# Seven block products for batches 1 and 2, with the sums of weights moved forward and batch 3 loaded into the first buffers

## The chip, the cores and the metric

The kernel runs on one core of one Trainium2 chip. The metric is the device time of one execution in microseconds (us). A core has a matrix engine (PE in the profile, with its weight loads as PEld), VectorE (DVE), ScalarE (ACT), GpSimd (POOL) and SyncE (SP, which here only issues transfers). Each engine works through its own queue of instructions in order; they wait for one another by semaphores.

## What is computed

Eight batches of linear attention with 8 heads, 576 positions and 64 numbers for each head, followed by an MLP mixer. Cut to what matters:

```
q_p, k_p = phi(q), phi(k)             # phi(x) = x + 1 for x > 0, exp(x) otherwise
kv  = einsum('bhsd,bhse->bhde', k_p, v)
num = einsum('bhsd,bhde->bhse', q_p, kv)
den = einsum('bhsd,bhd->bhs', q_p, k_p.sum(axis=2)) + 1e-6
x   = num / den                       # as [batch, 576, 512]
u   = x + token_mix(x)                # relu(x^T w_tok1) w_tok2, transposed back
out = u + relu(u @ w_ch1) @ w_ch2     # w_ch1 is 512 x 1536, w_ch2 is 1536 x 512
```

The change is about the last product, `relu(u @ w_ch1) @ w_ch2`, and about what has to be ready for it.

## The kernel before

The 576 positions of a batch are four tiles of 128 rows and a tail of 64. The tails of two neighbouring batches share one tile. Matrix operands are bfloat16, the sums in PSUM (eight banks of 512 floats) are float32.

**Stages and pieces.** The program is an order written out by hand. For each batch `n` there is a stage: a list `big` of pieces of matrix work of that batch, and a list `fill` of `(s, function)`. `run(big, fill)` emits piece 0, then what fill has at 0, then piece 1, and so on. Since engines work in order, this order is the order in every queue. The pieces of a stage are:

- `mm3(n, mc)` for 12 values of `mc` (L520): a 128-column slice of `relu(u @ w_ch1)`, four matmuls of 512 columns; ScalarE, or VectorE where `dve` is set, writes it from PSUM to `cr` (L532, L535).
- for odd `n`, three pieces `mm3_tail` (L537): the same for the shared tail.
- the product with `w_ch2`. For batches 0 to 2 it is `mm4(p, t, ...)` (L548): for a tile of rows 12 matmuls of 512 columns, cut into three pieces. For batches from 3 on (`FIRST = 3`, L595) it is `m4s(n)` (L713): 14 pieces of six matmuls of 256 columns.
- for odd `n`, three pieces of `mm4` for tile 8, the shared tail.

The stage named after batch 1 does `mm3` of batch 1, the `mm4` of batch 1's four tiles and the tail of batches 0 and 1 (L921). The stage of batch 2 does `mm3` and `mm4` of batch 2, and so on.

**The seven block products.** With the rows in even and odd tiles and the inner dimension in halves, `cr` is a 2 x 2 block matrix; so is `wc2` (w_ch2 in SBUF). Instead of eight products of blocks, `pair_product` (L680) makes seven, of sums of blocks. Four sums of blocks of `cr` are made for each batch by `row_sums(n, which, k0, m)` on VectorE (L621) and lie in `sb`. Four sums of blocks of the weights are made once, by `weight_sums` on GpSimd (L605), and lie in `tb`; a float32 helper `tf` serves three of them. Product 6 needs `sb[1]` and `tb[1]`, product 5 `sb[0]` and `tb[0]`, product 7 `sb[2]` and `tb[2]`, product 3 `sb[3]`, product 4 `tb[3]`; the order is 1, 2, 6, 5, 7, 3, 4. Three PSUM tiles X, Z, Y hold them. `pair_copy` (ScalarE, L695) saves an intermediate X or Y in `part`, `pair_end` (L698) adds the residual `u` on VectorE (L702) and the saved part on GpSimd (L704), `pair_put` (L706) sends the output off.

**Buffers.** `raw[nm, 0]` and `raw[nm, 1]` are two sets of float32 buffers for q, k and v. `rb(n)` (L123) says which set a batch is loaded into. `sb`, `tb`, `tf` and two of the `part` tiles have no space of their own: they lie in `raw["k", 1]`, `raw["q", 1]` and `raw["v", 1]` (L596 to L600) and in the spent `w2`. So seven products can be used only when the second set of buffers is free of inputs.

**What prepares a batch.** `phi_exp` (ScalarE, L148), `phi_add` (VectorE, L154) and `phi_end` (VectorE, L162) turn the loaded q or k, half a batch each, into `qp` or `kp`. `vcast` (L173) turns v into bfloat16. `kv(n)` (L181) multiplies kp and v in two groups of 36 small matmuls, the second of which uses the second halves. `qtr_dma` transposes q by a transfer. `nd_all(n)` (L249, "nd") makes numerators and denominators, and VectorE writes `x`. Then `mm1` (token mixing, L296), `mm2` in two parts a and b (L307), and transposing transfers `uta`, `utb` (L508), which give the next stage its input.

Of the kernel before, what the change touches and what calls it, by code (L numbers as in the profile page):

```python
# [12 lines left out]
ALU = mybir.AluOpType  # L13
# [5 lines left out]
def kernel(  # L19
# [20 lines left out]
    nc = tc.nc  # L40

    B, H, S, D = q.shape
# [11 lines left out]
    NCH = DCH // 128  # L54
# [63 lines left out]
    def after(ins, other):  # L118
        if other is not None:
            tc.add_manual_dep(ins.ins, other.ins.name, sync_dep, reason="order of transfers")  # L120
        return ins

    def rb(n):  # L123
        return n % 2 if n < 4 else 0

    def load(nm, n, c, gate=None):
        src_ = src[nm][n].rearrange("(j a) (p t) d -> (a p) j (t d)", a=2, t=T)
# [38 lines left out]
    def phi(nm, n, c):  # L166
        phi_exp(nm, n, 2 * c, 2)
        phi_add(nm, n, 2 * c, 2)
        phi_end(nm, n, 2 * c, 2)

    def vcast(n, c, copy=nc.scalar.copy):
        js = slice(2 * c, 2 * c + 2)
        copy(out=vs[:, js, :, 0:D],  # L173
             in_=raw["v", rb(n)][:, js].rearrange("p j (t d) -> p j t d", t=T))
# [41 lines left out]
    def qtr_dma(n):  # L216
        for a in range(2):
            nc.sync.dma_start_transpose(
                out=qT[n % 2][:, 2 * TD * a:2 * TD * (a + 1)].rearrange("p (f s) -> p f s", s=D),
                in_=qp[half[a]].rearrange("p c t i d -> p (c t i d)"))  # L220
# [299 lines left out]
    def mm3(n, mc, kjs=range(NDM), dve=False):  # L520
        b = n % 2
        if kjs[0] == 0:
            part_of[mc] = bank(None if n == 0 else (
                (0, 1, 0, 1, 2, 3, 0, 1, 2, 3, 0, 1) if n > 1 else
                (3, 5, 7, 1, 3, 0, 2, 1, 3, 0, 1, 0))[mc])
        ps = part_of[mc]
        for kj in kjs:
            nc.tensor.matmul(out=ps, lhsT=wc1[:, kj, 128 * mc:128 * mc + 128],  # L528
                             rhs=uT[b][:, :, kj],
                             start=(kj == 0), stop=(kj == NDM - 1))  # L530
        if kjs[-1] == NDM - 1 and dve:
            nc.vector.tensor_scalar(out=cr[b][:, mc, :], in0=ps, scalar1=0.0, scalar2=None,  # L532
                                    op0=ALU.max)
        elif kjs[-1] == NDM - 1:
            nc.scalar.activation(out=cr[b][:, mc, :], in_=ps, func=AF.Relu)  # L535

    def mm3_tail(i, late=True):  # L537
        ps = bank(((2, 3, 0) if late else (1, 2, 3))[i]).rearrange("p (m s) -> p m s", m=4)
        for m in range(4):
            mc = 4 * i + m  # L540
            for kj in range(NDM):
                nc.tensor.matmul(out=ps[:, m], lhsT=wc1[:, kj, 128 * mc:128 * mc + 128],  # L542
                                 rhs=uTt[:, kj, :], start=(kj == 0), stop=(kj == NDM - 1))
        nc.scalar.activation(out=crt[:, 4 * i:4 * i + 4, :], in_=ps, func=AF.Relu)
# [44 lines left out]
    KH = NCH // 2  # L589
# [2 lines left out]
        t = raw[nm, b].rearrange("p j f -> p (j f)").bitcast(BF16)  # L592
        return t[:, 1536 * i:1536 * (i + 1)]

    FIRST = 3  # L595
    tb = [bf("k", 1, i).rearrange("p (k c) -> p k c", k=KH) for i in range(3)] + [  # L596
        bf("q", 1, 0).rearrange("p (k c) -> p k c", k=KH)]
    tf = raw["q", 1].rearrange("p j f -> p (j f)")[:, 768:2304].rearrange("p (k c) -> p k c", k=KH)
# [3 lines left out]
    def wblock(i, j):  # L602
        return wc2[:, KH * i:KH * (i + 1), 256 * j:256 * (j + 1)]

    def weight_sums(k0, m):  # L605
        first = [live["phi"]]
        ks = slice(k0, k0 + m)
        b11, b12, b21, b22 = [wblock(i, j)[:, ks] for i in range(2) for j in range(2)]
        sub = lambda o, x_, y_: after(nc.gpsimd.tensor_tensor(
            out=o[:, ks], in0=x_, in1=y_, op=ALU.subtract), first.pop() if first else None)  # L610
        sub(tf, b12, b11)
        sub(tb[0], b12, b11)
        sub(tb[1], b22, tf[:, ks])
        sub(tb[2], b22, b12)
        sub(tf, b22, tf[:, ks])
        sub(tb[3], b21, tf[:, ks])

    def ablock(n, i, e):
        return cr[n % 2].rearrange("p k (j e s) -> p k j e s", j=2, e=2)[:, KH * i:KH * (i + 1), :, e]
# [93 lines left out]
    def m4s(n):  # L713
        if n + 1 < B:
            return [lambda i=i, j=j: pair_product(n, i, j) for i in ORDER for j in range(2)]
        out_ = []
        for e in LAST:
            out_ += [lambda e=e: product(n, e[1], e[0])] if e else m4(n // 2, [8])
        return out_

    def prep_k(n, g, copy=nc.scalar.copy):
        phi("k", n, g)
        vcast(n, g, copy)

    def k_exp(n):
        for g in range(2):
            phi_exp("k", n, 2 * g, 2)

    def load_all(n, nms):
        if n < B:  # L730
            for nm in nms:
                for g in range(2):
                    load(nm, n, g)
# [170 lines left out]
                 (en, lambda nm=nm, c=c: phi_end(nm, 1, 2 * c, 2))]  # L904
    late = [("vc", lambda: vcast(1, 0)), ("vc", lambda: vcast(1, 1, nc.vector.tensor_copy))]
    fill += [(21, lambda g=g: phi("q", 2, g)) for g in range(2)]
    fill += [(22, lambda: qtr_dma(2)), (22, lambda: load_all(3, "qkv"))]
    first = steps(1)
    for nm, fn in first[1:2] + late + first[2:3] + first[0:1] + first[3:]:
        fill += [(at0[nm], fn)]  # L910
# [7 lines left out]
    for mc in range(3):  # L918
        mm3(1, mc, range(0, 2))
    utr_tail(0)  # L920
    big = [lambda mc=mc: mm3(1, mc, range(2, 4)) for mc in range(3)] + [lambda mc=mc: mm3(1, mc, dve=mc in (5, 8)) for mc in range(3, NCH)] + [  # L921
        lambda i=i: mm3_tail(i, False) for i in range(3)] + m4(0, [4, 5, 6, 7, 8])
    at1 = {"nd": 10, "mm1": 16, "mm2a": 18, "mm2b": 20, "uta": 18, "utb": 20}
    fill = [(s, lambda g=g: phi("k", 2, g)) for g, s in ((0, 0), (1, 2))]
    fill += [(4, lambda: vcast(2, 0)), (5, lambda: vcast(2, 1, nc.vector.tensor_copy))]
    fill += [(8, lambda: kv(2, range(2)))]
    fill += [(at1[nm], fn) for nm, fn in steps(2)]
    fill += [(s, lambda g=g: phi("q", 3, g)) for g, s in ((0, 13), (1, 14))]
    fill += [(6, lambda: load_all(4, "k")), (15, lambda: qtr_dma(3)), (22, lambda: load_all(4, "qv"))]
    fill += [(s, lambda g=g: prep_k(3, g)) for g, s in ((0, 17), (1, 21))]  # L930
    fill += [(22, lambda: k_exp(4)), (22, lambda: weight_sums(0, 2)), (25, lambda: kv(3, range(2)))]
    run(big, sorted(fill, key=lambda e: e[0]))

    for n in range(2, B - 1):
        p, b = divmod(n, 2)
        blocks = n >= FIRST
        big = m3(n) + (m3t if b else []) + (m4s(n) if blocks else m4(p, [0, 1, 2, 3])) + (
            m4(p, [8]) if b else [])
        b0 = 15 if b else 12
        todo = dict(steps(n + 1))  # L940
        fill = []
        put = lambda s, fn: fill.append((s, fn))
        at = lambda s, *nms: [put(s, todo.pop(nm)) for nm in nms if nm in todo]
        sums = lambda s, w, k0, m: put(s, lambda: row_sums(n, w, k0, m)) if blocks else None
        on = lambda s, fn, *a: put(s, lambda: fn(*a)) if blocks else None
        more = n + 2 < B
        at(1, "nd")
        if more:
            for g in range(2):
                put(2, lambda g=g: phi_add("k", n + 2, 2 * g, 2))  # L950
                put(3 + g, lambda g=g: phi_end("k", n + 2, 2 * g, 2))
            put(5, lambda: load_all(n + 3, "k"))
            for g in range(2):
                put(7, lambda g=g: phi_exp("q", n + 2, 2 * g, 2))
            for g in range(2):
                put(8 + g, lambda g=g: phi_add("q", n + 2, 2 * g, 2))
                put(9 + g, lambda g=g: phi_end("q", n + 2, 2 * g, 2))
            put(10, lambda: qtr_dma(n + 2))
        at(7, "mm1")
        if n + 1 == FIRST:  # L960
            for i in (1, 2):
                put(10, lambda i=i: weight_sums(2 * i, 2))
        for s, k0 in ((11, 0), (12, 3)):
            for w in (1, 2):
                sums(s, w, k0, 3)
        at(13, "mm2a", "uta")
        sums(14, 3, 0, KH)
        at(b0 + 3 - b, "mm2b", "utb")
        sums(b0 + 4 - b, 4, 0, KH)
        on(b0 + 1, pair_copy, 0)  # L970
        if more:
            for g in range(2):
                put(b0 + 2 + g, lambda g=g: vcast(n + 2, g))
        on(b0 + 4 - b, pair_end, n, "Z", 0, 0, 0)
        on(b0 + 5, pair_copy, 1)
        at(b0 + 6, "mm2t", "utt")
        put(b0 + 6, lambda: load_all(n + 3, "qv"))
        on(b0 + 7, pair_copy, 2)
        if n + 3 < B:
            put(b0 + 8, lambda: k_exp(n + 3))  # L980
        if more:
            put(b0 + 9, lambda: kv(n + 2, range(2)))
        on(b0 + 9, pair_end, n, "X", 1, 1, 2)
        on(b0 + 11, pair_end, n, "Y", 0, 1, 1)
        on(b0 + 13, pair_end, n, "X", 1, 0)
        on(b0 + 13, pair_put, n)
        assert not todo, todo
        run(big, sorted(fill, key=lambda e: e[0]))

# [34 lines left out]
```

## Time and profile before

| | before |
|---|---|
| time, median of 3 (lowest to highest) | 254.04 us (253.87 to 254.38) |
| span of the profiled execution | 252.8 us |
| PE busy | 244.1 us, 97% of the span |
| DVE, ACT, POOL busy | 161.3, 138.3, 68.0 us |
| granted TensorE clock | 1.00 |

PE busy for 97% of the span says that there are hardly any gaps between its instructions, not that each of them is at its best. The engines beside it have much idle time on average, but it is unevenly spread. The profile is read here mostly by stage: in the chain of work that ended last, the stage of batch 1 begins at about 54 us, that of batch 2 at 85.66, of batch 3 at 112.56 and of batch 4 at 142.89. A name such as `k_raw` in a row is a buffer of the program; where weight sums or row sums lie in it, the row shows the buffer's name.

### The profile page before, as it was taken

To read this page: it belongs to the slowest core of one execution; us is meant where nothing else is said; L and a number is where in the kernel's file an instruction comes from. 1 tells how busy PE (TensorE), PEld (TensorE's weight loads), DVE (VectorE), ACT (ScalarE), POOL (GpSimd) and SP (SyncE) were. 2 spreads that over 40 slices of the span, in tenths; PEclk is the share of its full clock that TensorE was granted. 3 is DMA by queue.
4 is the path that set the end of the run, shared out by engine and by line. 5 is a ranking of instruction groups with operands and counts; after the bars stand their busy time and mean duration, and the time that the engine had idled before them with its cause. 6 is when DMAs were issued, how large, how long until landed. Compare 5 with 4: busy or idle time off the path is not lost.

```text
span 252.8 us, 5704 instructions
## 1 busy us (share of the span) xinstructions
PE 244.1 (97%) x2358; PEld 144.6 (57%) x2358; DVE 161.3 (64%) x282; ACT 138.3 (55%) x218; POOL 68.0 (27%) x84
## 2 busy tenths in 40 slices
PE   7689999999999999999999999999999999999993
PEld 3474455554744444444588545774578545764872
DVE  5855877876876394648854398939864444833543
ACT  4674782469684369416967168566863165137300
POOL 9670120120005904981003500150004500160000
PEclk9999999999999999999999999999999999999999
DMA  6999999899938966459786957769252540435034
GB/s 248 262 203 263 364 233 337 304 269 340 377 94 146 325 223 223 104 163 342 272 126 178 327 136 204 151 200 346 41 114 44 111 100 0 86 62 124 3 93 114
DMA packets 49769, 48.37 MB, mean 191 GB/s; under 512 B 30096, under 2 KB 35600, under 8 KB 49744
## 3 DMA queue, kind: packets, MB, share of 16 engines
q1 hardware_dynamic: 41568, 34.87, 46.6%
q0 software_dynamic: 7632, 12.49, 22.6%
q10 hardware_dynamic: 544, 0.66, 1.1%
q8 instruction: 18, 0.29, 0.4%
q14 instruction: 7, 0.06, 0.1%
HBM read 35.85 MB, written 9.44 MB: 179 GB/s over the span
## 4 chain that ended last, share of the span: by engine, by line
PE 90%; DMA 3%; ACT 2%; DVE 2%; issue 1%; SPq 0%; DVEq 0%; ACTq 0%
PE ps L528 33%; PE ps L555 16%; PE ps L691 15%; PE ps L302 6%; PE ps L542 4%; PE ps L315 4%; PE ps L644 4%; DMA q_raw<-in_q_dram 3%; PE ps L188 2%; PE ps L258 2%; PE ps L463 1%; PE ps L473 1%; PE ps L354 1%; PE ps L336 1%; PE ps L229 0%
## 5 line engine op out<-in xcount | busy, mean ns | idle before, releaser
L528 PE MATMUL ps<-uT,wc 128*128 128x512 bf16 x384 | 87.2, 379 | 0.0
L535 ACT ACTIVATE cr<-ps 128x512 bf16<-128x512 f32 x91 | 53.4, 601 | 44.4 <-PE ps L528 43.9
L528 PEld LDWEIGHTS <-wc 128*128 128x128 bf16 x384 | 36.8, 98 | 43.5 <-issue 1.5
L555 PE MATMUL ps<-wc,cr 128*128 128x512 bf16 x144 | 34.3, 379 | 0.0
L704 POOL TENSOR_TENSOR obuf<-obuf,q_raw 128x512 f32<-128x512 f32 x4 | 5.1, 1263 | 77.3 <-ACT w L696 58.8
L148 ACT ACTIVATE e<-q_raw 128x1152 bf16<-128x1152 f32 x16 | 18.1, 1159 | 7.3 <-DMA q_raw<-in_q_dram 6.7
L555 PEld LDWEIGHTS <-cr 128*128 128x128 bf16 x144 | 13.4, 98 | 14.7 <-issue 0.4
L327 DVE TENSOR_TENSOR u<-ps,x 128x1024 bf16<-128x1024 f32 x12 | 14.7, 1224 | 10.6 <-PE ps L315 10.4
L626 DVE TENSOR_TENSOR v_raw<-cr 128x768 bf16<-128x768 bf16 (+1 forms) x15 | 10.3, 687 | 15.8 <-ACT cr L535 15.8
L148 ACT ACTIVATE e<-k_raw 128x1152 bf16<-128x1152 f32 x16 | 18.2, 1165 | 2.7 <-DMA k_raw<-in_k_dram 2.7
L702 DVE TENSOR_TENSOR obuf<-ps,u 128x512 f32<-128x512 f32 x16 | 11.0, 689 | 12.4 <-PE ps L691 9.5
L577 POOL DMA_DIRECT2D out_dram<-obuf x12 | 7.3, 613 | 42.1 <-DVE obuf L572 42.1
L271 DVE TENSOR_TENSOR x<-ps,dens 128x768 bf16<-128x768 f32 x18 | 17.2, 958 | 0.6
L691 PE MATMUL ps<-k_raw,v_raw 128*128 128x256 bf16 x144 | 16.7, 273 | 0.0
L691 PEld LDWEIGHTS <-cr 128*128 128x128 bf16 x144 | 14.0, 98 | 2.9
L691 PEld LDWEIGHTS <-v_raw 128*128 128x128 bf16 x144 | 13.9, 98 | 2.8 <-issue 0.8
L302 PE MATMUL ps<-x,w 128*128 128x512 bf16 x56 | 14.4, 379 | 0.0
L162 DVE TENSOR_TENSOR qp<-e,y 128x1152 bf16<-128x1152 bf16 x16 | 12.1, 758 | 2.2 <-ACT e L148 0.9
L173 ACT CAST vs<-v_raw 128x1152 bf16<-128x1152 f32 x12 | 13.5, 1162 | 0.0
L572 DVE TENSOR_TENSOR obuf<-ps,u 128x512 f32<-128x512 f32 x12 | 8.2, 688 | 7.9 <-PE ps L555 7.8
L162 DVE TENSOR_TENSOR kp<-e,y 128x1152 bf16<-128x1152 bf16 x16 | 11.7, 752 | 2.1 <-ACT e L148 1.9
L315 PE MATMUL ps<-ar,w2p 128*128 128x512 bf16 x50 | 12.9, 379 | 0.0
(132 smaller groups left out, 350.2 us busy)
## 6 DMA issues: line engine op xcount, KB each, us to landing
k_raw<-in_k_dram SPq DMA_DIRECT2D x16, 576.0 KB, 7.2
q_raw<-in_q_dram SPq DMA_DIRECT2D x16, 576.0 KB, 5.7
v_raw<-in_v_dram SPq DMA_DIRECT2D x14, 576.0 KB, 9.1
out_dram<-obuf POOLq DMA_DIRECT2D x8, 512.0 KB, 6.7
wc<-in_moe_w_ch_dram POOLq DMA_DIRECT2D x8, 384.0 KB, 9.9
out_dram<-obuf POOLq DMA_DIRECT2D x12, 256.0 KB, 6.5
out_dram<-obuf POOLq DMA_DIRECT2D x6, 128.0 KB, 5.6
cr<-in_v_dram POOLq DMA_DIRECT2D x2, 288.0 KB, 8.1
```

Of the source, the lines that this page charges most:

```text
L148: nc.scalar.activation(out=e, in_=f, func=AF.Exp)
L162: live["phi"] = nc.vector.tensor_tensor(out=dst.transpose([0, 2, 1, 3]), in0=e.rearrange("p (i t d) -> p i t d", i=nj, t=T), in1=y.rearran ...
L173: copy(out=vs[:, js, :, 0:D], in_=raw["v", rb(n)][:, js].rearrange("p j (t d) -> p j t d", t=T))
L271: nc.vector.tensor_tensor(out=xv[:, :, rc0:rc0 + 3], in0=v_[:, :, k0:k0 + 6, 0:D].rearrange("p i (q a) d -> p i q a d", a=2), in1=den[:, : ...
L302: nc.tensor.matmul(out=ps[:, mt], lhsT=w1t[:, b, ms] if r == R else w1[:, r, ms], rhs=x[b][:, r, :], start=(r == 0), stop=(r == R))
L315: nc.tensor.matmul(out=ps[:, i], lhsT=w2v(kt, r, b), rhs=ar[b][:, kt, :], start=(kt == 0), stop=(kt == NT - 1 and not add))
L327: nc.vector.tensor_tensor(out=u[b][:, rs[0]:rs[0] + m], in0=ps[:, 0:m], in1=x[b][:, rs[0]:rs[0] + m], op=ALU.add)
L528: nc.tensor.matmul(out=ps, lhsT=wc1[:, kj, 128 * mc:128 * mc + 128], rhs=uT[b][:, :, kj], start=(kj == 0), stop=(kj == NDM - 1))
L535: nc.scalar.activation(out=cr[b][:, mc, :], in_=ps, func=AF.Relu)
L555: nc.tensor.matmul(out=ps, lhsT=crt[:, kc, :] if t == 8 else cr[b][:, kc, 128 * r:128 * r + 128], rhs=wc2[:, kc, :], start=(kc == 0), stop ...
L691: nc.tensor.matmul(out=live[tile_][:, j], lhsT=lhs[:, k_], rhs=rhs[:, k_], start=(first and j == 0 and k_ == 0), stop=(k_ == KH - 1), skip ...
L702: nc.vector.tensor_tensor(out=o, in0=live[tile_], in1=u[n % 2][:, d::2, HC[c]], op=ALU.add)
```

## The change

Batches 1 and 2 use the seven block products too. For that the sums of weights have to be ready two stages earlier, and the second set of buffers has to be free earlier, so batch 3 goes into the first set. Only batch 1 uses the second set now.

```diff
     def rb(n):
-        return n % 2 if n < 4 else 0
+        return 1 if n == 1 else 0
...
-    FIRST = 3
...
+    B11, B12, B21, B22 = [wblock(i, j) for i in range(2) for j in range(2)]
+    def weight_sums(*abc):
+        first = [live["phi"]]
+        for o, x_, y_ in abc:
+            for k0 in range(0, KH, 2):
+                ks = slice(k0, k0 + 2)
+                after(nc.gpsimd.tensor_tensor(out=o[:, ks], in0=x_[:, ks], in1=y_[:, ks],
+                                              op=ALU.subtract), first.pop() if first else None)
+    def weight_sum(o, x_, y_):
+        nc.vector.tensor_tensor(out=o, in0=x_, in1=y_, op=ALU.subtract)
...
-    fill += [(22, lambda: qtr_dma(2)), (22, lambda: load_all(3, "qkv"))]
+    fill += [(22, lambda: qtr_dma(2)), (22, lambda: load_all(3, "q"))]
+    fill += [(22, lambda: weight_sums((tf, B12, B11), (tb[1], B22, tf)))]
```

The GpSimd sums run in two groups of six instructions: two of the sums near the end of the stage of batch 0, as above, and `tf` again and `tb[3]` in the stage of batch 1. `tb[0]` and `tb[2]` are made by VectorE. The stage of batch 1, cut to what is spoken of below:

```diff
-    big = ... + [lambda i=i: mm3_tail(i, False) for i in range(3)] + m4(0, [4, 5, 6, 7, 8])
+    big = ... + [lambda i=i: mm3_tail(i, False) for i in range(3)] + m4s(1) + m4(0, [8])
+    put(0, phi_exp, "k", 2, 0, 2)
+    put(0, phi_add, "k", 2, 0, 2)
+    put(0, phi_add, "k", 2, 2, 2)
+    put(0, weight_sum, tb[0], B12, B11)
+    put(1, phi_end, "k", 2, 0, 2)
+    put(2, phi_exp, "k", 2, 2, 2)
+    put(2, weight_sum, tb[2], B22, B12)
+    put(3, phi_end, "k", 2, 2, 2)
+    put(3, weight_sums, (tf, B22, tf), (tb[3], B21, tf))
+    put(3, load_all, 3, "k")
+    put(4, vcast, 2, 0)
+    put(5, vcast, 2, 1, nc.vector.tensor_copy)
+    put(6, load_all, 3, "v")
+    put(8, kv, 2, range(2))
+    put(10, todo["nd"])
...
+    put(16, pair_copy, 0)
+    put(16, todo["mm1"])
+    put(17, row_sums, 1, 3, 0, KH)
+    for g in range(2):
+        put(17 + g, vcast, 3, g)
...
+    put(21, pair_end, 1, "Z", 0, 0, 0)
...
+    put(22, k_exp, 3)
+    put(24, pair_end, 1, "X", 1, 1, 2)
+    for g in range(2):
+        put(24, phi_add, "k", 3, 2 * g, 2)
+    put(25, load_all, 4, "k")
+    put(26, pair_end, 1, "Y", 0, 1, 1)
+    for g in range(2):
+        put(27, phi_end, "k", 3, 2 * g, 2)
+    put(28, pair_end, 1, "X", 1, 0)
+    put(28, pair_put, 1)
+    put(29, kv, 3, range(2))
```

In the loop over the later stages `m4s(n)` is used throughout. The preparation of k for batch 4 moves to pieces 10 to 14 of the stage of batch 2 (it was at the start of that stage), that of k and q for batch 5 to pieces 7 to 10 and 12 to 14 of the stage of batch 3, with their loads and casts moved to suit. From the stage of batch 4 on the order is the old one.

More of the change, by code (lines that the diff above doesn't have):

```diff
@@ L603, in wblock @@
         return wc2[:, KH * i:KH * (i + 1), 256 * j:256 * (j + 1)]
-    def weight_sums(k0, m):
+    B11, B12, B21, B22 = [wblock(i, j) for i in range(2) for j in range(2)]
+    def weight_sums(*abc):
         first = [live["phi"]]
[L607 to L616, printed above, removed]
+        for o, x_, y_ in abc:
[5 more added lines that the diff above has]
+        nc.vector.tensor_tensor(out=o, in0=x_, in1=y_, op=ALU.subtract)
     def ablock(n, i, e):
@@ L920 @@
     utr_tail(0)
[L921 to L931, printed above, removed]
+    big = [lambda mc=mc: mm3(1, mc, range(2, 4)) for mc in range(3)] + [
+        lambda mc=mc: mm3(1, mc, dve=mc in (5, 8)) for mc in range(3, NCH)] + [
+        lambda i=i: mm3_tail(i, False) for i in range(3)] + m4s(1) + m4(0, [8])
@@ new lines @@
+    fill = []
+    put = lambda s, fn, *a: fill.append((s, lambda: fn(*a)))
+    todo = dict(steps(2))
+    put(0, phi_exp, "k", 2, 0, 2)
[9 more added lines that the diff above has]
+    put(4, vcast, 2, 0)
@@ new lines @@
+    put(5, vcast, 2, 1, nc.vector.tensor_copy)
+    put(6, load_all, 3, "v")
+    put(8, kv, 2, range(2))
+    put(10, todo["nd"])
+    for s, k0 in ((11, 0), (12, 3)):
+        for w in (1, 2):
+            put(s, row_sums, 1, w, k0, 3)
+    for g in range(2):
+        put(12 + g, phi_exp, "q", 3, 2 * g, 2)
+        put(13, phi_add, "q", 3, 2 * g, 2)
+        put(14, phi_end, "q", 3, 2 * g, 2)
+    put(15, qtr_dma, 3)
+    put(16, pair_copy, 0)
+    put(16, todo["mm1"])
+    put(17, row_sums, 1, 3, 0, KH)
@@ new lines @@
+    for g in range(2):
+        put(17 + g, vcast, 3, g)
+    put(19, todo["mm2a"])
+    put(19, todo["uta"])
+    put(20, row_sums, 1, 4, 0, KH)
+    put(20, pair_copy, 1)
+    put(21, pair_end, 1, "Z", 0, 0, 0)
+    put(21, todo["mm2b"])
+    put(21, todo["utb"])
+    put(22, load_all, 4, "qv")
+    put(22, pair_copy, 2)
+    put(22, k_exp, 3)
[4 more added lines that the diff above has]
+    put(26, pair_end, 1, "Y", 0, 1, 1)
@@ L932 @@
+    for g in range(2):
+        put(27, phi_end, "k", 3, 2 * g, 2)
+    put(28, pair_end, 1, "X", 1, 0)
+    put(28, pair_put, 1)
+    put(29, kv, 3, range(2))
     run(big, sorted(fill, key=lambda e: e[0]))
@@ L935 @@
         p, b = divmod(n, 2)
-        blocks = n >= FIRST
-        big = m3(n) + (m3t if b else []) + (m4s(n) if blocks else m4(p, [0, 1, 2, 3])) + (
-            m4(p, [8]) if b else [])
+        big = m3(n) + (m3t if b else []) + m4s(n) + (m4(p, [8]) if b else [])
         b0 = 15 if b else 12
@@ L941, with phi_at @@
         fill = []
-        put = lambda s, fn: fill.append((s, fn))
+        put = lambda s, fn, *a: fill.append((s, lambda: fn(*a)))
         at = lambda s, *nms: [put(s, todo.pop(nm)) for nm in nms if nm in todo]
-        sums = lambda s, w, k0, m: put(s, lambda: row_sums(n, w, k0, m)) if blocks else None
-        on = lambda s, fn, *a: put(s, lambda: fn(*a)) if blocks else None
-        more = n + 2 < B
-        at(1, "nd")
[L948 to L958, printed above, removed]
+        def phi_at(nm, ex, ad, en):
+            for g in range(2):
+                if ex is not None:
+                    put(ex[g], phi_exp, nm, n + 2, 2 * g, 2)
+            for g in range(2):
+                put(ad[g], phi_add, nm, n + 2, 2 * g, 2)
+                put(en[g], phi_end, nm, n + 2, 2 * g, 2)
@@ new lines @@
+        at(1, "nd")
+        if n + 2 < B:
+            if n > 3:
+                phi_at("k", None, (2, 2), (3, 4))
+                put(5, load_all, n + 3, "k")
+            if n != 3:
+                phi_at("q", (7, 7), (8, 9), (9, 10))
+            else:
+                phi_at("k", (7, 7), (8, 9), (9, 10))
+            put(10, *((qtr_dma, n + 2) if n != 3 else (load_all, n + 3, "k")))
+            if n == 2:
+                for g in range(2):
+                    put(10, phi_add, "k", n + 2, 2 * g, 2)
@@ L959 @@
         at(7, "mm1")
-        if n + 1 == FIRST:
-            for i in (1, 2):
-                put(10, lambda i=i: weight_sums(2 * i, 2))
         for s, k0 in ((11, 0), (12, 3)):
             for w in (1, 2):
-                sums(s, w, k0, 3)
+                put(s, row_sums, n, w, k0, 3)
+        if n == 3:
+            phi_at("q", (12, 13), (13, 13), (14, 14))
+            put(15, qtr_dma, n + 2)
         at(13, "mm2a", "uta")
-        sums(14, 3, 0, KH)
+        put(14, row_sums, n, 3, 0, KH)
@@ L968 @@
+        put(b0 + 1, pair_copy, 0)
+        if n == 2:
+            for g in range(2):
+                put(b0 + 1, phi_exp, "k", n + 2, 2 * g, 2)
+                put(b0 + 2, phi_end, "k", n + 2, 2 * g, 2)
+            put(b0 + 4, load_all, n + 3, "k")
         at(b0 + 3 - b, "mm2b", "utb")
-        sums(b0 + 4 - b, 4, 0, KH)
-        on(b0 + 1, pair_copy, 0)
-        if more:
+        put(b0 + 4 - b, row_sums, n, 4, 0, KH)
+        put(b0 + 4 - b, pair_end, n, "Z", 0, 0, 0)
+        put(b0 + 5, pair_copy, 1)
@@ L972 @@
+        if n + 2 < B:
             for g in range(2):
-                put(b0 + 2 + g, lambda g=g: vcast(n + 2, g))
-        on(b0 + 4 - b, pair_end, n, "Z", 0, 0, 0)
-        on(b0 + 5, pair_copy, 1)
+                put(b0 + (5 if n == 2 else 2) + g, vcast, n + 2, g)
         at(b0 + 6, "mm2t", "utt")
[L977 to L986, printed above, removed]
+        put(b0 + 7, load_all, n + 3, "qv")
+        put(b0 + 7, pair_copy, 2)
+        if n > 2 and n + 3 < B:
+            put(b0 + 8, k_exp, n + 3)
+        if n + 2 < B:
+            put(b0 + 9, kv, n + 2, range(2))
+        put(b0 + 9, pair_end, n, "X", 1, 1, 2)
+        put(b0 + 11, pair_end, n, "Y", 0, 1, 1)
+        put(b0 + 13, pair_end, n, "X", 1, 0)
@@ L987 @@
+        put(b0 + 13, pair_put, n)
         assert not todo, todo
```

## The prediction

> **What bounds the kernel now.** I read the busy shares first, then the chain of work that ended last, then the busy time by stage, and last the timelines of VectorE, ScalarE, GpSimd and SyncE from 44 to 145 us. From the page, and from the busy time by stage (the columns are PE, PEld, DVE, ACT, POOL, clock, DMA share, GB/s):
>
> ```profile
> PE 244.1 (97%) x2358; PEld 144.6 (57%) x2358; DVE 161.3 (64%) x282; ACT 138.3 (55%) x218; POOL 68.0 (27%) x84
> PE 90%; DMA 3%; ACT 2%; DVE 2%; issue 1%; SPq 0%; DVEq 0%; ACTq 0%
> ```
>
> ```profile
> 53.96:85.66 31.70, 31.70 (x357) 16.57 (x358) 20.96 (x34) 21.76 (x31) 8.13 (x10) 1.00 0.84 252
> 85.66:112.56 26.90, 26.90 (x231) 12.39 (x230) 16.33 (x27) 14.99 (x22) 17.62 (x19) 1.00 0.61 188
> 112.56:142.89 30.33, 30.33 (x324) 19.71 (x322) 19.52 (x32) 18.44 (x28) 6.62 (x8) 1.00 0.87 256
> 142.89:168.61 25.72, 25.72 (x268) 15.93 (x266) 20.11 (x33) 16.65 (x25) 4.05 (x5) 1.00 0.68 160
> ```
>
> The reader is to see that PE is busy for the whole of each stage, 31.70 of 31.70 us. So time goes only if PE gets less to do, and comes only if PE is made to wait. And stages 2 and 4 have the same pieces but for the product with w_ch2: 26.90 us with 48 wide matmuls, 25.72 us with seven block products.
>
> From the chain in order of time (start, us, what), the two products and the place where kv(2) runs:
>
> ```profile
> 60.98 0.71 PE ps L188 x68
> ...
> 67.89 1.73 PE ps L555 x8
> ...
> 76.96 4.32 PE ps L555 x20
> ...
> 132.29 4.58 PE ps L691 x42
> ```
>
> 4.32/20 = 0.216 us for a 512-column matmul, 4.58/42 = 0.109 us for a 256-column one.
>
> VectorE and then GpSimd, from the timeline:
>
> ```profile
> 56.56 0.76 DVE L162 TENSOR_TENSOR kp<-e,y 128x1152 bf16<-128x1152 bf16 x1 [0.82 <-ACT e L148]
> 57.24 0.75 DVE L154 TENSOR_SCALAR y<-k_raw 128x1152 bf16<-128x1152 f32 x1
> 58.59 0.76 DVE L162 TENSOR_TENSOR kp<-e,y 128x1152 bf16<-128x1152 bf16 x1 [0.60 <-ACT e L148]
> 59.26 0.68 DVE L532 TENSOR_SCALAR cr<-ps 128x512 bf16<-128x512 f32 x1
> 59.86 0.75 DVE L173 CAST vs<-v_raw 128x1152 bf16<-128x1152 f32 x1
> ```
>
> ```profile
> 80.96 1.15 POOL L609 TENSOR_TENSOR k_raw<-wc 128x512 bf16<-128x512 bf16 x1
> 82.07 1.16 POOL L609 TENSOR_TENSOR k_raw<-wc,q_raw 128x512 bf16<-128x512 bf16 x1
> 137.81 1.27 POOL L704 TENSOR_TENSOR obuf<-obuf,part 128x512 f32<-128x512 f32 x1 [1.40 <-DVE obuf L702]
> ```
>
> The cast for kv(2) ends at 60.61, 0.3 us before kv(2) starts: VectorE has little slack there. Sums on GpSimd start every 1.12 us.
>
> [...] The trace of before can't confirm this for sums: wherever a GpSimd sum runs (79.8 to 86.7, 98.1 to 111.7, and L704), the VectorE instructions beside it are those from PSUM (L572, L582, L327, L340, L702), and they keep their length (L572 0.69). A weak sign is a GpSimd transfer issue that began at 30.83 beside L154 and took 0.90 against 0.74 and 0.76 for the next two. [...]
>
> **The change part by part.**
>
> *The products.* For two batches 48 x 0.216 = 10.37 becomes 84 x 0.109 = 9.18, 1.19 less each. The stages agree: 26.90 - 25.72 = 1.18. Twice that is 2.36. Without any new wait: 254.04 - 2.36 = 251.68.
>
> *First group on GpSimd.* Six sums after phi_end of q2, which ends at 48.05: 6 x 1.12 = 6.7, to 54.8. VectorE then has L572, L359, L372, L323, each from PSUM, so no lock; the next L154 is at 54.99. Behind the sums on GpSimd wait batch 0's output transfers (49.84 moves to 54.8, the last to 57.3); their obuf slots are not written again before stage 2. Cost 0.
>
> *Stage 1, start.* With the distances of the rows (L154 and L162 0.67, 1536-element sum 0.87, L532 0.67) VectorE does from 54.99: y, y, tb[0] to 57.20, phi_end to 57.87, tb[2] to 58.74, phi_end (exp ends at 58.56) to 59.41, the L532 of piece 5 to 60.08, then the cast to 60.84. The two sums, 1.9 us, fill the old gaps (0.82, 0.60, 0.40). kv(2) starts at 60.98 and needs this cast in its second half, 0.35 later at 61.3. But the second GpSimd group starts at 59.5, when phi_end ends, and its first sum runs to about 60.7. The cast [...] would wait, run 60.7 to 61.45, and hold PE 0.2. If the lock costs nothing, 0; if the cast loses a second turn, it ends at 62.6 and PE loses 1.3. I take 0.2. Behind the cast are L532 of piece 8 and nd's VectorE part at 63.95, both with slack.
>
> *Row sums, mm1.* nd's x is ready at 68.47; mm1 comes after two narrow pieces instead of two wide ones, at 67.89 + 1.31 = 69.2: free. The second GpSimd group ends by 67.5, before row_sums (68.4 on) and pair_copy(0) at about 69.8, which overwrites tf. Row sums 4 x 0.56 + 2 x 0.95 = 4.1, beside PE; product 6 wants its sum at 72.7 (done 70.8), product 7 at 77.0 (done 74.3), product 3 at 78.3 (done 76.3). The three ACT copies (0.59) and three POOL adds (1.27) lie beside PE. Cost 0.
>
> *Loads.* k3 waits for exp of k2 (58.6), v3 for the cast of v2 (61.5). v loads take 9.1 (median), so v3 is there at 70.6; its casts stand on ScalarE at about 71.7. q4, v4 and k4 go out by 82.5 and are needed from 92 on. uT of batch 2 is complete 6 us ahead of stage 2. Cost 0.
>
> *Stage 1, end.* PE by pieces: 24 ends at 78.34, 26 at 79.65, 28 at 80.96, 29 at 81.8, then kv(3). VectorE: pair_end X from 78.38, phi_add of k3 at 78.98 and 79.65, pair_end Y at 80.32, phi_end from 80.92, the second from 81.6 to 82.35. kv(3)'s second half wants it at 82.2, so 0.2 is lost without any lock. With it, GpSimd's add for X is due at 79.2 while phi_add holds the lock. VectorE starts the next phi_add before the last is done (0.67 apart, 0.75 long), so I take it to keep the lock: the add runs 80.4 to 81.67, and phi_end, two SBUF inputs, is held from 80.92 to 81.67. The two end at 82.42 and 83.1. The first half of kv(3) waits 81.8 to 82.47, the second 82.83 to 83.15: 1.0 lost. If the two engines take turns instead, phi_end number two also waits for the add for Y (1.27): it ends at 84.45 (2.3 lost), or at 85.1 if GpSimd also gets in between the two phi_add (3.0 lost). I take 1.0, bounds 0.2 and 3.0.
>
> *Stages 2 and 3.* The sums leave GpSimd there (18 x 1.12 us), which were hidden. Stage 2 becomes like stage 4 on PE, with two phi_add and two phi_end more between rows that matter: row sum for product 6 ready 15.1 us into the stage against 17.6 wanted, product 7 17.5 against 20.8, product 3 20.8 against 22.8; kp 18.8 and vs 21.7 against kv(4) at 22.1. Stage 3 likewise: 15.1 against 20.3, 19.8 against 22.9, 21.8 against 25. No phi stands beside a GpSimd add there. Cost 0.
>
> Sum: 254.04 - 2.36 + 0.2 + 1.0 = 252.88; I say 252.8.
>
> **The rivals.** (1) The lock is not felt, or short: only the gap of 0 to 0.3 at kv(3) remains, 251.7 to 252.0. For it: no VectorE row of before is stretched beside GpSimd work by more than 0.3 us (L154, 1.03 at 32.76). Against it: no pair of that kind occurs. (2) The two engines take strict turns: 254.04 - 2.36 + 0.2 + 2.3 to 3.0 = 254.2 to 254.9, and up to 1.1 more if the cast loses twice; no gain, or slower. For it: GpSimd's add is already waiting when phi_end asks. Against it: VectorE's back-to-back starts. (3) v3 is late: the slowest v load took 14.6; issued at 61.4 it lands at 76.0, two casts of 1.1 stand before pair_copy(1), which ends at 78.8 where product 7 wants it at 77.0: 1.8 more, 254.6. Against it: no load of batch 4 competes in those microseconds any more (before, three loads of k and v stood in line).
>
> **How the numbers follow.** VectorE keeping the lock, 252.8: 0.37. Rival 1: 0.33. Rival 2: 0.25, of which 0.10 falls within 0.2% (253.53 to 254.55) and 0.15 above. Rival 3: 0.05, above. Faster 0.70, same 0.10, slower 0.20. The range runs from 251.6 (no wait at all) to 254.7 and leaves out the upper part of rivals 2 and 3.
>
> **What would show it.** L555 falls from 192 to 96 matmuls, L691 rises from 336 to 504. PE in stage 2 takes 25.7. PE has a gap before the L188 groups near 61 and 82 and nowhere else; their sum is the time less 251.68. The cast at about 60 and phi_end at about 81 wait for a GpSimd instruction, which starts or ends at that moment. I am wrong if PE waits at mm1 or at products 6, 7 or 3 (row sums late), at an L148 or L173 that waits for a transfer, or if the VectorE rows near 48 to 55 grow.

## The result and the profile after

The changed kernel takes 256.07 us (median of 4, 255.84 to 256.32), the kernel before in the same comparison 254.07. The ratio is 1.0078, 95% interval 1.006 to 1.0095: slower, where 252.8 was forecast. From the page of the changed kernel:

```profile
PE 244.3 (96%) x2430; PEld 152.4 (60%) x2430; DVE 172.1 (68%) x296; ACT 141.2 (55%) x224; POOL 69.2 (27%) x80
PEclk9999999999999799999999999999999999999999
PE 85%; DVE 5%; DMA 3%; ACT 3%; issue 2%; SPq 0%; DVEq 0%; ACTq 0%
```

Two things are new. VectorE has 5% of the chain of work that ended last, it had 2%. And the granted clock has one dip, in slice 14 of 40. The busy time by stage says where (stages 1 to 4, then the 3.5 us behind kv(3); columns as before):

```profile
53.66:88.52 34.86, 32.49 (x393) 20.57 (x394) 28.46 (x42) 21.19 (x32) 16.95 (x16) 0.95 0.75 233
88.52:114.24 25.72, 25.72 (x268) 15.90 (x266) 19.95 (x33) 16.65 (x25) 4.04 (x5) 1.00 0.61 164
114.24:144.57 30.33, 30.33 (x324) 19.72 (x322) 19.45 (x32) 20.32 (x30) 7.19 (x8) 1.00 0.88 264
144.57:170.29 25.72, 25.72 (x268) 15.91 (x266) 20.12 (x33) 16.65 (x25) 4.02 (x5) 1.00 0.64 178
85.05:88.52 3.47, 3.47 (x9) 1.19 (x10) 0.06 (x1) 0.75 (x2) 1.27 (x2) 0.53 1.03 402
```

Stage 2 went from 26.90 to 25.72 us: the products gave their 1.18. Stage 3 is unchanged. All of the loss is in stage 1, 34.86 us for 31.70 before, and PE was busy for only 32.49 of it. PE's timeline at the end of stage 1, and at kv(2) near its start:

```profile
60.62 1.05 PE L188 MATMUL ps<-vs,kp 64*64 64x65 bf16 x72
...
80.76 1.03 PE L555 MATMUL ps<-wc,crt 128*128 128x512 bf16 x4
82.83 0.48 PE L188 MATMUL ps<-vs,kp 64*64 64x65 bf16 x36 [1.04 <-DVE kp L162]
84.56 0.48 PE L188 MATMUL ps<-vs,kp 64*64 64x65 bf16 x36 [1.25 <-DVE kp L162]
84.98 3.54 PE L555 MATMUL ps<-wc,crt 128*128 128x512 bf16 x8
```

kv(2) is stretched from 0.78 to 1.05. kv(3) waits twice for phi_end of k3 (`kp L162`), 1.04 + 1.25 = 2.29 us. Then eight matmuls take 3.48 us by the chain, where eight took 1.73 before: they ran at about half clock (0.53 from 85.05 to 88.52). VectorE and then GpSimd in the same places:

```profile
59.72 1.41 DVE L173 CAST vs<-v_raw 128x1152 bf16<-128x1152 f32 x1
61.05 0.68 DVE L532 TENSOR_SCALAR cr<-ps 128x512 bf16<-128x512 f32 x1
...
79.02 2.49 DVE L154 TENSOR_SCALAR y<-k_raw 128x1152 bf16<-128x1152 f32 x2
81.43 0.68 DVE L701 TENSOR_TENSOR obuf<-ps,u 128x512 f32<-128x512 f32 x1
82.03 2.48 DVE L162 TENSOR_TENSOR kp<-e,y 128x1152 bf16<-128x1152 bf16 x2
```

```profile
59.35 7.28 POOL L611 TENSOR_TENSOR q_raw<-wc,q_raw 128x512 f32<-128x512 bf16 x6 [1.91 <-DVE kp L162]
...
79.25 1.65 POOL L703 TENSOR_TENSOR obuf<-obuf,part 128x512 f32<-128x512 f32 x1 [0.94 <-DVE obuf L701]
82.19 1.71 POOL L703 TENSOR_TENSOR obuf<-obuf,w 128x512 f32<-128x512 f32 x1 [1.29 <-DVE obuf L701]
```

A pair of phi instructions took 1.42 us before; each pair takes 2.5 here. The first of a pair keeps its length (0.75 and 0.74); the second, shown here by itself, does not:

```profile
79.68 1.82 DVE L154 TENSOR_SCALAR y<-k_raw 128x1152 bf16<-128x1152 f32 x1
82.70 1.81 DVE L162 TENSOR_TENSOR kp<-e,y 128x1152 bf16<-128x1152 bf16 x1
```

The two engines alternate: phi_add to 79.77, GpSimd's add (its row begins at 79.25, while phi_add is still running) to 80.90, the second phi_add to 81.50, and the same again with phi_end and the add for Y. Such a wait of one engine for the other's instruction is what the prediction calls the lock; there it was an assumption of its author. An instruction from PSUM kept its length beside GpSimd: L532 at 61.05 took 0.68 us while the weight sums ran.

The sum of these terms accounts for the time: 254.07 - 2.36 for the products + 0.27 at kv(2) + 2.29 at kv(3) + 1.75 for the clock = 256.02, measured 256.07.

### The profile page after: what moved, and what is told of

It is laid out like the page before. It is cut to its first block, busy times and chain, and to the rows that moved or that the text cites. A ratio compares the mean times of both kernels' runs of the same rounds, so it can differ in the third digit from the quotient of the medians.

```text
span 254.5 us, 5882 instructions
## 1 busy us (share of the span) xinstructions
PE 244.3 (96%) x2430; PEld 152.4 (60%) x2430; DVE 172.1 (68%) x296; ACT 141.2 (55%) x224; POOL 69.2 (27%) x80
## 4 chain that ended last, share of the span: by engine, by line
PE 85%; DVE 5%; DMA 3%; ACT 3%; issue 2%; SPq 0%; DVEq 0%; ACTq 0%
PE ps L528 30%; PE ps L690 21%; PE ps L555 8%; PE ps L302 6%; PE ps L542 4%; PE ps L315 4%; PE ps L643 4%; DMA q_raw<-in_q_dram 3%; PE ps L188 2%; PE ps L258 2%; DVE kp L162 2%; PE ps L463 1%; ACT e L148 1%; PE ps L473 1%; PE ps L354 1%
## 5 line engine op out<-in xcount | busy, mean ns | idle before, releaser
L703 POOL TENSOR_TENSOR obuf<-obuf,q_raw 128x512 f32<-128x512 f32 x6 | 7.6, 1268 | 107.0 <-ACT w L695 76.9
L701 DVE TENSOR_TENSOR obuf<-ps,u 128x512 f32<-128x512 f32 x24 | 16.5, 689 | 14.3 <-PE ps L690 11.3
L690 PE MATMUL ps<-k_raw,v_raw 128*128 128x256 bf16 x216 | 25.4, 273 | 0.0
L625 DVE TENSOR_TENSOR v_raw<-cr 128x768 bf16<-128x768 bf16 (+1 forms) x21 | 14.4, 687 | 16.2 <-ACT cr L535 16.2
L690 PEld LDWEIGHTS <-v_raw 128*128 128x128 bf16 x216 | 20.9, 98 | 4.7 <-issue 1.2
L690 PEld LDWEIGHTS <-cr 128*128 128x128 bf16 x216 | 21.0, 98 | 4.3
L690 PE MATMUL ps<-wc,cr 128*128 128x256 bf16 x144 | 17.7, 273 | 0.0
L162 DVE TENSOR_TENSOR kp<-e,y 128x1152 bf16<-128x1152 bf16 x16 | 12.8, 818 | 2.8 <-ACT e L148 2.6
L162 DVE TENSOR_TENSOR qp<-e,y 128x1152 bf16<-128x1152 bf16 x16 | 11.9, 756 | 3.8 <-ACT e L148 3.0
L154 DVE TENSOR_SCALAR y<-k_raw 128x1152 bf16<-128x1152 f32 x16 | 12.7, 820 | 2.3 <-DMA k_raw<-in_k_dram 2.3
L173 ACT CAST vs<-v_raw 128x1152 bf16<-128x1152 f32 x12 | 13.4, 1162 | 0.0
L555 PE MATMUL ps<-wc,crt 128*128 128x512 bf16 x48 | 12.8, 419 | 0.0
L154 DVE TENSOR_SCALAR y<-q_raw 128x1152 bf16<-128x1152 f32 x16 | 12.1, 765 | 0.2 <-DMA q_raw<-in_q_dram 0.2
```

Of the source, the lines that this page charges most:

```text
L154: nc.vector.tensor_scalar(out=y, in0=f, scalar1=1.0, scalar2=1.0, op0=ALU.add, op1=ALU.max)
L162: live["phi"] = nc.vector.tensor_tensor(out=dst.transpose([0, 2, 1, 3]), in0=e.rearrange("p (i t d) -> p i t d", i=nj, t=T), in1=y.rearran ...
L555: nc.tensor.matmul(out=ps, lhsT=crt[:, kc, :] if t == 8 else cr[b][:, kc, 128 * r:128 * r + 128], rhs=wc2[:, kc, :], start=(kc == 0), stop ...
L690: nc.tensor.matmul(out=live[tile_][:, j], lhsT=lhs[:, k_], rhs=rhs[:, k_], start=(first and j == 0 and k_ == 0), stop=(k_ == KH - 1), skip ...
L701: nc.vector.tensor_tensor(out=o, in0=live[tile_], in1=u[n % 2][:, d::2, HC[c]], op=ALU.add)
```

## The experiments

The theory after the result: VectorE and GpSimd take turns, this makes kv(3) wait, and the gaps on PE make its clock fall. Rival A: VectorE simply has too much to do at the end of stage 1. Rival B: the clock falls for a reason of its own.

**Adds moved behind phi.** The two GpSimd adds of stage 1 that stood beside phi_add and phi_end now wait for the last phi_end. Work, engines and buffers are the same. With `True` as its last argument `pair_end` leaves its add to `pair_late`.

```diff
+    def pair_late():
+        for o, i in live.pop("late"):
+            after(nc.gpsimd.tensor_tensor(out=o, in0=o, in1=part[i], op=ALU.add), live["phi"])
...
-    put(24, pair_end, 1, "X", 1, 1, 2)
+    put(24, pair_end, 1, "X", 1, 1, 2, True)
-    put(26, pair_end, 1, "Y", 0, 1, 1)
+    put(26, pair_end, 1, "Y", 0, 1, 1, True)
...
+    put(27, pair_late)
```

> Theory: at the end of the stage of batch 1 the GpSimd adds for X and Y and VectorE's four phi instructions of k3 take turns [...]; that holds kv(3) for 2.3 us, and these gaps make the TensorE clock fall to half, 1.75 us more. With the two adds behind the last phi_end, phi_add and phi_end keep 0.75 us each, kv(3) waits 0.2 to 0.5 us, no matmul of 0.43 us follows: 256.07 - 1.9 - 1.75 = 252.4. Rival A, VectorE has too much to do there whatever GpSimd does: phi_end still ends near 84.5, time 256. Rival B, the clock falls for a reason of its own (the load of the stage): only the wait goes, 254.1.

Measured: 252.22 us, ratio to before 0.993 (0.9914 to 0.9947). VectorE's timeline, then PE's (the added lines move the numbers: L705 is what was L701):

```profile
78.60 1.42 DVE L154 TENSOR_SCALAR y<-k_raw 128x1152 bf16<-128x1152 f32 x2
79.93 0.68 DVE L705 TENSOR_TENSOR obuf<-ps,u 128x512 f32<-128x512 f32 x1
80.53 1.42 DVE L162 TENSOR_TENSOR kp<-e,y 128x1152 bf16<-128x1152 bf16 x2
```

```profile
81.34 0.48 PE L188 MATMUL ps<-vs,kp 64*64 64x65 bf16 x36
82.00 0.48 PE L188 MATMUL ps<-vs,kp 64*64 64x65 bf16 x36 [0.18 <-DVE kp L162]
82.42 1.90 PE L555 MATMUL ps<-wc,crt 128*128 128x512 bf16 x8
```

Both pairs are back at 1.42, one wait of 0.18 is left, and the eight matmuls run at full clock (1.90 us for 3.54). The order of two GpSimd instructions alone was worth about 3.8 us (256.07 - 252.22). Rival A falls: VectorE does the same work in time. Rival B's 254.1 does not fit either.

**The same, and weight sums behind the cast.** The second GpSimd group starts behind the VectorE cast of v2 (`"vc"`) instead of the last phi_end.

```diff
-    put(3, weight_sums, (tf, B22, tf), (tb[3], B21, tf))
+    put(5, lambda: weight_sums((tf, B22, tf), (tb[3], B21, tf), behind="vc"))
```

> As the run with late adds, and the second GpSimd group of weight sums waits for the VectorE cast of v2 instead of phi_end of k2. Theory: the cast at about 59.7 goes back from 1.41 to 0.75 us and the 0.25 us that PE waits in kv(2) goes too: 0.25 less than the run with late adds, about 252.1. Rival: the wait in kv(2) comes from the order on VectorE[...]: no difference between the two runs.

Measured: 251.94 us, ratio 0.9922 (0.9907 to 0.9936), 0.28 less than the run before it. The two intervals overlap, so the times alone do not separate the two; the rows do: the cast is back at 0.75, and kv(2) at 0.78.

```profile
59.38 0.75 DVE L173 CAST vs<-v_raw 128x1152 bf16<-128x1152 f32 x1
```

**The gaps filled.** The changed kernel, with added matmuls where PE waits; their results are not used.

```diff
         for c in cs:
+            for _ in range(fill[c]):
+                nc.tensor.matmul(out=psum[:, 6], lhsT=wc1[:, 0, 0:128], rhs=wc1[:, 0, 0:512],
+                                 start=True, stop=True)
...
-    put(29, kv, 3, range(2))
+    put(29, kv, 3, range(2), (5, 6))
```

> The changed kernel with 5 matmuls of 512 columns ahead of the first half of kv(3) and 6 between its halves, into a free bank, so that PE has work while it waits (their results are not used). Theory: VectorE and GpSimd still take turns, phi_end ends as late as before, kv(3) ends as late, but the clock stays full and the eight matmuls behind it take 1.73 instead of 3.48 us: 254.3. Rival B, the clock does not follow the gaps: 256.1, with 0.43 us matmuls again.

Measured: 254.54 us, ratio 1.0023 (1.0016 to 1.003), against 1.0078. PE's timeline (L187 are the added matmuls, L191 is kv, L558 is what was L555):

```profile
81.42 1.24 PE L187 MATMUL ps<-wc 128*128 128x512 bf16 x5
82.62 0.48 PE L191 MATMUL ps<-vs,kp 64*64 64x65 bf16 x36
83.04 1.47 PE L187 MATMUL ps<-wc 128*128 128x512 bf16 x6
84.44 0.48 PE L191 MATMUL ps<-vs,kp 64*64 64x65 bf16 x36
84.85 1.90 PE L558 MATMUL ps<-wc,crt 128*128 128x512 bf16 x8
```

VectorE and GpSimd alternate as before and kv(3) ends as late, but the eight matmuls behind it keep full clock (1.90 us; mean granted clock 0.996 to 1.0 in the 17 executions). So 1.5 us of the loss (256.07 to 254.54) came from PE having nothing to do while it waited, and not from the later end of kv(3). Rival B falls.

**kv(3) two pieces later.**

```diff
-    put(29, kv, 3, range(2))
+    put(31, kv, 3, range(2))
```

> kv(3) two pieces later, at 31 instead of 29; nothing else moved. Theory: the turns on VectorE and GpSimd stay as they are, but kv(3) asks 1.73 us later: the first half does not wait, the second waits about 0.65, the clock does not fall: 256.07 - 1.64 - 1.75 = 252.7. Rival B: only the wait goes, 254.4.

Measured: 252.88 us, ratio 0.9953 (0.9938 to 0.9969). The pairs on VectorE still take 2.5 us; kv(3) waits once, 0.64 us, and the clock stays full (0.998 to 1.0 in the 4 executions). The slow phi costs only what of it reaches PE.

```profile
84.34 0.48 PE L188 MATMUL ps<-vs,kp 64*64 64x65 bf16 x36 [0.64 <-DVE kp L162]
```

**Both repairs, kv(3) at 30.**

> Late adds, the gated weight sums, and kv(3) one piece later, at 30. In the run with the first two, PE still waits about 0.3 us for phi_end of k3. Theory: kv(3) asks 0.86 us later, this wait goes too, and nothing waits from 54 us on: 251.94 - 0.3 = 251.65, which is 254.0 less the 2.36 us of the products. Rival: kv(3) later makes its copy on ScalarE or nd(3) late, and the time stays at 251.9 or above.

Measured: 251.57 us, ratio 0.9906 (0.9889 to 0.9922). It beats both kernels. Between 54 and 110 us no wait of PE for another engine is left in its list of waits, and the gain, 2.4 us by the ratio and 2.47 by the medians (254.04 - 251.57), is about what the products alone should give (2.36).

**A gap without contention.** On the kernel with both repairs, kv(3) at 29 again, the first matmul of kv(3) waits for a late GpSimd add, for X (short gap, shown) or for Y (long gap, with `live["add", 1]`).

```diff
+                    if gate is not None:
+                        after(mm, gate)
+                        gate = None
...
-    put(29, kv, 3, range(2))
+    put(29, lambda: kv(3, range(2), live["add", 2]))
```

> The kernel with late adds and gated sums, and the first matmul of kv(3) made to wait for the late GpSimd add for X, which ends at about 83.1: one unbroken gap on PE of about 1.7 us and no contention of VectorE and GpSimd. If the clock falls after any gap of over 1.2 us: 251.94 + 1.4 + 1.75 = 255.1. If it needs nearly 3 us with little work: no 0.43 us matmuls, 253.3.

> The same with the wait on the add for Y, which ends at about 84.35: one gap of about 2.9 us. Theory that the gaps alone make the clock fall: half-clock matmuls of 0.43 us for some microseconds behind kv(3), 251.94 + 2.6 + 1.7 = 256.2, without any lock. Rival B, the clock fell for another reason ([...]the load of the stage): full-clock matmuls, 254.5.

Measured, short: 253.77 us, ratio 1.0003 (0.9989 to 1.0018). The single times fall into two groups: 13 of 18 between 253.56 and 254.21, 5 between 255.20 and 255.59. The profiled execution is of the upper group. Its PE waits 1.98 us, and the clock halves at the end of kv(3):

```profile
83.24 0.78 PE L188 MATMUL ps<-vs,kp 64*64 64x65 bf16 x72 [1.98 <-POOL obuf L703]
84.35 3.17 PE L558 MATMUL ps<-wc,crt 128*128 128x512 bf16 x7 [0.33 <-issue]
```

Measured, long: 257.27 us, two runs (256.56 and 257.97), ratio 1.013 (1.0097 to 1.0164). The profiled one is the first; it has half-clock matmuls behind a gap of 3.19 us. The second took 1.4 us more at a lower mean clock (0.983 against 0.993); there is no trace of it, so why stays open.

```profile
84.70 1.21 PE L188 MATMUL ps<-vs,kp 64*64 64x65 bf16 x72 [3.19 <-POOL obuf L703]
```

The stretches at half clock, in the changed kernel and with the short and the long gap (columns as in the busy time by stage; the clock is the third number from the end):

```profile
84.93:88.34 3.41, 3.41 (x24) 1.17 (x11) 0.18 (x1) 0.75 (x2) 1.27 (x2) 0.50 1.04 402
83.96:87.38 3.42, 3.09 (x16) 1.22 (x10) 0.00 (x0) 0.75 (x2) 1.72 (x3) 0.50 1.04 406
84.58:88.00 3.42, 2.96 (x77) 1.86 (x79) 0.00 (x0) 0.75 (x2) 1.33 (x3) 0.50 1.04 398
```

Each lasts 3.4 us, and each begins some 3 us after the end of the last wide matmul before kv(3): 3.1 us after 81.79, 2.7 after 81.26, 3.1 after 81.51. In that time the changed kernel and the one with the short gap did nearly all of the 72 small matmuls of kv(3), the one with the long gap none. The longest single wait does not decide it: it is 1.25 us in the changed kernel, where the clock fell in all 4 executions, and 1.98 with the short gap, where it fell in 5 of 18. The waits together (2.29 against 1.98) fit that order, and so may the whole stretch without wide matmuls; no run here separates these two.

Neither of these kernels has VectorE and GpSimd in each other's way at that point, and the clock falls in both. So a gap is enough, and with the gaps filled the same alternation left the clock full: the two engines' turns reach the clock only by way of the gap. Neither of the two answers expected for the short gap was right: it makes the clock fall in some executions and not in others.

## Why the prediction was wrong

- *The products*: right. Stage 2 gave 1.18, and the kernel with both repairs and kv(3) at 30 has the whole gain (2.4 by the ratio).
- *First group on GpSimd, row sums, mm1, loads, stages 2 and 3, all at nothing*: right. Stage 2 takes 25.72 us on PE as foretold, stage 3 30.33 as before; VectorE's L359 at 49 to 51 us kept its 0.69; no wait at mm1, at products 3, 6 or 7 or for a transfer shows on PE.
- *Stage 1, start*: right. The two sums of 1536 elements on VectorE took 0.94 and 0.95 us (L626 in the trace of before: 0.95), with the next start 0.86 and 0.87 us later, as taken there. The cast lost one turn, 1.41 for 0.75, and PE 0.27 where 0.2 was taken.
- *Stage 1, end*: here the step failed that said "VectorE starts the next phi_add before the last is done (0.67 apart, 0.75 long), so I take it to keep the lock". It did not. In both pairs GpSimd got in between, although VectorE's next instruction had begun 0.08 us before the last one ended. That is the order of rival 2's upper case, priced there at 3.0. The wait was 2.29 where the forecast took 1.0: once phi had ended, GpSimd's add was through in 1.1 us (79.77 to 80.90, 82.77 to 83.90) instead of 1.27, and the held phi in 0.6 instead of 0.75. That 2.29 is also the figure of rival 2's lower case (2.3) is chance, since the order was the other one. The prediction's own figures put the add first: due at 79.2, with the second phi_add at 79.65. In the trace, too, the add's row begins first, at 79.25 and 82.19 against 79.68 and 82.70, and so does the weight sum's (59.35) before the cast's (59.72). So the rows fit "who asked first goes first" as well as "strict turns"; no run here separates the two. The 0.2 that the prediction took for this place without any lock was right: 0.18 and 0.19 are left with the adds moved.
- *Missing from every case*: the clock. The forecast and all rivals priced gaps on PE at their own length, and none gave a reason for that. These cost 1.75 us on top, which takes the time past rival 2's 254.2 to 254.9 and past the end of the range. The granted clock was at half from 84.93 to 88.34, 3.41 us. What sets off such a fall, and what ends it, was not shown: PE was idle here for 2.29 us in two parts, with 36 small matmuls between the two waits, and with the long gap, where PE had nothing at all to do, the clock fell after 3.1 us.

That VectorE and GpSimd hold each other up is shown by the rows and by moving two instructions; why they do was not shown. Beside GpSimd's sums and adds the cast took 1.41 us, the second phi_add 1.82 and the second phi_end 1.81, where the cast of v2 takes 0.75 in the trace of before and the first of each pair 0.75 and 0.74 here; instructions from PSUM kept 0.68 (L532 at 61.05) and 0.69 (L359).

## What to carry to other kernels

When PE has no gaps, a new wait costs its length and perhaps a fall of the clock as well. Here waits of 2.29 us in two parts and of 3.19 us brought one in each execution, and a wait of about 2 us in some; a wait of 0.64 us brought none. Price it so, or fill the wait with other matmuls, or put what waits later in the order. Look for GpSimd arithmetic beside VectorE instructions of the kinds that were held here: a cast and a tensor_scalar from SBUF to SBUF (L173, L154) and a tensor_tensor with both inputs in SBUF (L162). Each waited until the GpSimd instruction was through, the cast 0.66 us and phi 1.07, and GpSimd's adds took 1.65 and 1.71 us instead of 1.27, even though one engine's instructions stood back to back. Order alone cured it here: what PE does not wait for started behind what PE needs.

## What the runs showed of the hardware that had not been expected

- Back-to-back instructions on VectorE did not keep GpSimd out: with starts 0.67 us apart and 0.75 us long, a GpSimd add of 1.27 us got in between, and the second VectorE instruction's row grew to 1.82.
- A waiting instruction counts as busy in the profile: the stretched rows (1.41, 1.65, 1.71, 1.82) hold the wait for the other engine, and no line of the list of waits names it.
- The clock of the matrix engine fell in all 4 executions of the changed kernel (mean granted clock 0.990 to 0.993; in no execution without such gaps was it under 0.996), with gaps of 1.04 and 1.25 us around 36 small matmuls, in 5 executions of 18 where PE waited once (1.98 us in the profiled one), and in both with the gap of 3.19 us. In the three profiled falls the clock was at half for 3.4 us; in the changed kernel a 512-column matmul then took 0.43 us (3.48/8) instead of 0.216.
